# Attention and two expert layers on one core: POOL normalises with a one-input operation and rounds two weights itself

## The chip, the cores and the metric

The kernel runs on one core of a Trainium2 chip. Times are device microseconds (us) of that core. The engines are TensorE (PE in the profile; PEld is its weight load), VectorE (DVE), ScalarE (ACT), GpSimd (POOL) and SyncE (SP), which here only issues DMAs. Of the kernel before, three runs were timed; of every kernel one execution was also recorded by the hardware profiler, and that one has its own time.

## What is computed

The reference works in float32 on shapes that don't change (2 batches, 12 heads, 448 positions, 64 values a head, 896 tokens of 768):

```
scores = q @ k.T / sqrt(64), causal mask, minus the row's maximum
attn   = exp(scores);  attn = attn / (sum(attn) + 1e-9)
x      = attn @ v, heads side by side            # 896 x 768
h      = ((x @ w1) * (x @ w2)) @ w3              # 896 x 1024
x2     = h @ w_out                               # 896 x 768
h2     = x2 @ w_in;  g = h2 * clip(h2 + 3, 0, 6) / 6
out    = g @ w_out2
```

All weights arrive as 64-bit floats and are turned into 32-bit ones on the chip.

## The kernel before

[...]

**Weights.** A unit of a weight is fetched by one DMA as pairs of 32-bit words (`fetch`). `bits` makes a float32 of each pair: ACT scales the high word (line 270), DVE shifts the low word (line 277) and joins the two in two operations (lines 279 and 281). The result lies in the low word's place, so every second 32-bit word is a result. `split` then has ACT round it to `hi` (line 252) and has DVE or POOL subtract for `lo` (line 255). For the names in `POOLED`, `wr` (8 units of 128x768, the first `w_out`) and `w3` (8 units of 128x1024), the subtraction is POOL's.

**Attention.** Twelve units of two heads run first. For each, PE makes seven blocks of scores with 64 to 448 columns (line 407), DVE masks them and takes the row's extreme (line 410), ACT takes the exponential with its row sum (line 414), DVE adds 1e-9 and inverts the sums in three groups of rows (lines 425 and 426; the groups are the blocks of 448 and 384, of 320 and 256, and of 192, 128 and 64 columns), POOL multiplies each block by its inverse (line 433), PE transposes (line 455), ACT and DVE copy out of PSUM (lines 463 and 467), PE multiplies by v (line 480), and ACT and DVE split the result (lines 497 and 498). Line 433 is a `tensor_tensor` whose second operand is one value for each partition, repeated along the row.

**Beside it.** The product of `w3` and the first `w_out` (`weights_product`, called pw: 8 parts of 48 matmuls of 128x384, line 543) doesn't depend on attention. Its matmuls have a rank behind all of attention's and fill PE's gaps; what is left runs after attention. The products of x with w1 and w2 (line 686), by Strassen's scheme, come next, then lines 760, 625 and 801.

**Order.** Nothing in the program is issued as it is written. Each step is handed to `Plan` with an engine, a cost from a formula of the number of columns, what it reads and writes, and a rank. `Plan.issue` plays the engines forward by these costs and issues, on whichever engine is free, the step of lowest rank that is ready. A changed cost, or a step on another engine, therefore moves instructions on all engines. Every engine then works its queue in order, and semaphores hold it where it is early.

```
    def act(n, sb=False):
        return (0.29 if sb else 0.16) + n * 0.000833
    def dve(n):
        return 0.155 + n * 0.00104
    def pool(n):
        return 0.15 + n * 0.0023
```

Of the kernel before, what the change touches and what calls it, by code (L numbers as in the profile page):

```python
# [154 lines left out]
def attention_moe_moe2(ctx: ExitStack, tc, q, k, v, w1, w2, w3, w_out, v_in, v_out, out):  # L155
# [64 lines left out]
# [6 lines that stand above are left out]
    def pool(n):  # L226
        return 0.15 + n * 0.0023

    def fetch(plan, n, rank):
        if n >= len(units):  # L230
            return
        w, kt, m, name = units[n]
        size = kt * P
        if name == "w2":
            raw = plan.tile(lambda: later["t"].tile([P, KD * P, 2], U32, tag="raw2", name=f"{name}r{m}", bufs=2),
                            "raw2", 2, (done,))
            raw2s.append(raw)
        else:
            raw = plan.tile(lambda: ws.tile([P, KF * P, 2], U32, tag="raw", name=f"{name}r{m}", bufs=RAWS), "raw", RAWS)
        raws[n] = (raw, size)  # L240
        flat = lambda: raw[:, :size].rearrange("p f t -> p (f t)")
        if name == "wp":
            plan.op("sp", size * 0.0015, lambda: nc.sync.dma_start(flat()[:, :size], product_of[m].bitcast(U32)),
                    reads=[made], writes=[raw], rank=rank)
        else:
            plan.op("sp", size * 0.0029, lambda: nc.sync.dma_start(flat(), w[m].bitcast(U32)),
                    writes=[raw], rank=rank)

    def split(plan, hl, at_, size, x, reads, rank, eng="dve"):

        key = ("h", at_)
        plan.op("act", act(size, True), lambda: nc.scalar.copy(hl[:, HI, at_:at_ + size], x()),
                reads=reads, writes=[hl.at(("h", at_))], rank=rank)
        e = nc.gpsimd if eng == "pool" else nc.vector
        plan.op(eng, pool(size) if eng == "pool" else dve(size), lambda: e.tensor_tensor(  # L255
            hl[:, LO, at_:at_ + size], x(), f32(hl[:, HI, at_:at_ + size]), ALU.subtract),
            reads=[*reads, hl.at(("h", at_))], writes=[hl.at(("l", at_))], rank=rank)
# [1 line left out]
    def parts(name, m):  # L259
        return plan.tile(lambda: ws.tile([P, 2, KF * P], F32R, tag="hl", name=f"{name}{m}", bufs=HLS), "hl", HLS)  # L260

    def bits(plan, raw, size, rank, shifted=False):

        hi = lambda: raw[:, :size, 1]
        lo = lambda: raw[:, :size, 0]
        hb, lb = raw.at("h"), raw.at("l")

        plan.op("act", act(size, True), lambda: nc.scalar.mul(hi().bitcast(F32), hi().bitcast(F32), 2.0 ** -112),  # L270
                writes=[hb], rank=rank)
        if shifted:
            plan.op("act", act(size, True), lambda: nc.scalar.activation(
                lo(), lo(), AF.Copy, bias=THIRD[1], scale=THIRD[0]), writes=[lb], rank=rank)
        else:
            plan.op("dve", 0.16 + size * 0.00052,
                    lambda: nc.vector.tensor_single_scalar(lo(), lo(), 29, ALU.logical_shift_right),
                    writes=[lb], rank=rank)
        plan.op("dve", dve(size), lambda: nc.vector.scalar_tensor_tensor(  # L279
            lo(), hi(), 3, lo(), ALU.logical_shift_left, ALU.bitwise_or), reads=[hb], writes=[lb], rank=rank)  # L280
        plan.op("dve", dve(size), lambda: nc.vector.scalar_tensor_tensor(  # L281
            lo(), hi(), 0x80000000, lo(), ALU.bitwise_and, ALU.bitwise_or), reads=[hb], writes=[lb], rank=rank)

    def convert(plan, n, rank):
        if n >= len(units):
            return
        w, kt, m, name = units[n]
        if name == "w1":
            return
        raw, size = raws.pop(n)  # L290
        if name == "w2":
            combine(plan, m, raws.pop(n - 1)[0], raw, rank)
            return
        if name == "wr":
            hl = plan.tile(lambda: wrp.tile([P, 2, KD * P], F32R, tag="wr", name=f"wr{m}", bufs=KF), "wr", KF)
        else:
            hl = parts(name, m)
        hls[n] = hl
        if name == "wp":
            x = lambda: f32(raw[:, :].rearrange("p f t -> p (f t)")[:, :size])  # L300
            split(plan, hl, 0, size, x, [raw], rank)
            return
        bits(plan, raw, size, rank)
        split(plan, hl, 0, size, lambda: f32(raw[:, :size, 0]), [raw.at("l")], rank,
              "pool" if name in POOLED else "dve")

    def combine(plan, f, r1, r2, rank):

# [110 lines left out]
    def normalise(u, t0, t1):  # L419
# [10 lines left out]
        def scale(t):  # L430
            n = (t + 1) * T
            s = pb[:, OFF[t]:OFF[t] + n]
            nc.gpsimd.tensor_tensor(s, s, sm[:, 1, t:t + 1].to_broadcast([P, n]), ALU.mult)  # L433

        for t in reversed(range(t0, t1)):
            plan.op("pool", pool((t + 1) * T), lambda t=t: scale(t),
                    reads=[sm.at((1, t))], writes=[pb.at(t)], rank=rank)


# [431 lines left out]
```

## Time and profile before

| | |
|---|---|
| median of 3 runs | 581.37 us (580.28 to 582.85) |
| the profiled execution | 580.64 us |
| its span, first to last instruction | 578.9 us |
| PE busy | 555.5 us, 96% |
| DVE busy | 401.4 us, 69% |
| ACT busy | 294.5 us, 51% |
| POOL busy | 150.2 us, 26% |
| mean granted clock of TensorE | 0.994 |

The busy times are unions of instructions, so they can't exceed a stretch's length. They are averages over stages that are limited by different engines: POOL has work in the first half alone, and almost all of it in attention. Matmuls overlap one another, so the mean time of one is longer than the time that it adds. Where an engine's operation is held inside the hardware, not by a semaphore, the profile shows a longer operation and no wait.

### The profile page before, as it was taken

Reading aid. Unit: us, or ns where it says so; the run is one execution under the profiler, and the core shown is the slowest. Engines: PE = TensorE matmul, PEld = TensorE weight load, DVE = VectorE, ACT = ScalarE, POOL = GpSimd, SP = SyncE. Lnnn points to the kernel's source line nnn. Section 1 sums busy time; section 2 is a strip of 40 time slices with the busy share of each in tenths; the row PEclk is TensorE's granted clock in tenths of the full one; section 3 lists DMA queues with packets and bytes.
Section 4 is the critical chain, followed back from the end, with each engine's and each line's share of the span. In section 5 each row is a group of like instructions: output and inputs, shape, how many; then the busy total and the mean of one; then the engine's idle time right before and its main releaser. Section 6 shows DMA issues by size and latency. Waiting matters only on the chain.

```text
span 578.9 us, 7881 instructions
## 1 busy us (share of the span) xinstructions
PE 555.5 (96%) x2900; PEld 493.8 (85%) x2900; DVE 401.4 (69%) x675; ACT 294.5 (51%) x548; POOL 150.2 (26%) x143
## 2 busy tenths in 40 slices
PE   7697979899999999999999999999999999999997
PEld 5465656678899999889999999999999999999996
DVE  5979898897794799999736357877878855361000
ACT  5777778777673576665514335555555623130100
POOL 3968787697131243332100000000000000000000
PEclk9889999999999999999999999999999999999999
DMA  8655565543432233431413204333344442430000
GB/s 329 218 176 176 200 233 205 178 166 130 134 113 64 93 120 127 143 133 44 140 60 110 84 25 163 110 109 110 110 145 146 145 162 89 173 110 16 17 32 33
DMA packets 22855, 73.39 MB, mean 127 GB/s; under 512 B 2080, under 2 KB 11296, under 8 KB 20256
## 3 DMA queue, kind: packets, MB, share of 16 engines
q1 hardware_dynamic: 22816, 72.88, 36.6%
q8 instruction: 23, 0.38, 0.3%
q14 instruction: 16, 0.13, 0.1%
HBM read 66.98 MB, written 5.90 MB: 126 GB/s over the span
## 4 chain that ended last, share of the span: by engine, by line
PE 72%; DVE 16%; POOL 4%; issue 4%; DMA 2%; ACT 1%; SPq 0%; DVEq 0%; POOLq 0%; ACTq 0%
PE po L801 20%; PE pg L625 20%; PE px L760 10%; PE pw L543 9%; POOL prb L433 4%; PE s L407 3%; PE ptp L455 3%; PE paX L686 3%; DVE wd L255 2%; PE o L480 2%; DVE z L410 2%; DVE w1r L279 2%; PE paZ L686 1%; DMA ks<-in_k 1%; PE paY L686 1%
## 5 line engine op out<-in xcount | busy, mean ns | idle before, releaser
L801 PE MATMUL po<-g,vo 128*128 128x448 f32 x576 | 115.4, 362 | 0.0
L625 PE MATMUL pg<-x2t,vi 128*128 128x448 f32 x576 | 115.4, 362 | 0.0
L625 PEld LDWEIGHTS pg<-x2t,vi 128*128 128x128 f32 x576 | 108.0, 187 | 7.2
L801 PEld LDWEIGHTS po<-g,vo 128*128 128x128 f32 x576 | 108.0, 187 | 7.2
L433 POOL TENSOR_TENSOR prb<-prb,sums 128x448 f32<-128x448 f32 (+6 forms) x84 | 74.3, 911 | 27.5 <-DVE sums L426 25.3
L543 PE MATMUL pw<-wr,w 128*128 128x384 f32 x384 | 76.1, 347 | 0.5 <-POOL wr L255 0.5
L543 PEld LDWEIGHTS pw<-wr,w 128*128 128x128 f32 x384 | 65.9, 188 | 2.5 <-POOL wr L255 0.7
L407 PE MATMUL s<-ks,qs 128*128 128x448 f32 (+6 forms) x168 | 49.8, 405 | 10.5 <-DVE sums L410 9.8
L760 PE MATMUL px<-ab,wp 128*128 128x448 f32 x288 | 57.9, 362 | 0.0
L760 PEld LDWEIGHTS px<-ab,wp 128*128 128x128 f32 x288 | 54.0, 187 | 3.6
L414 ACT ACTIVATE prb<-z,sums 128x448 f32<-128x448 f32 (+6 forms) x84 | 42.3, 509 | 7.2 <-DVE sums L410 7.1
L407 PEld LDWEIGHTS s<-ks,qs 128*128 128x128 f32 x168 | 27.5, 192 | 19.3 <-DVE sums L410 14.2
L410 DVE CUSTOM_DVE_ANT_0 z<-s,maskb 128x448 f32<-128x448 f32 (+6 forms) x84 | 32.9, 418 | 11.5 <-PE s L407 7.3
L646 ACT ACTIVATE r<-pg,consts 128x448 f32<-128x448 f32 x32 | 20.3, 635 | 33.2 <-PE pg L625 33.2
L455 PEld LDWEIGHTS ptp<-ident,prb 128*128 128x128 f32 x192 | 23.0, 146 | 13.6 <-POOL prb L433 8.6
L455 PE MATMUL ptp<-ident,prb 128*128 128x128 f32 x192 | 27.8, 288 | 6.1 <-POOL prb L433 6.1
L270 ACT ACTIVATE vor<-vor 128x1024 f32<-128x1024 f32 x12 | 13.9, 1162 | 38.7 <-DMA vor<-in_moe_w_out 38.7
L463 ACT COPY pt<-ptp 128x512 f32<-128x512 f32 (+1 forms) x48 | 25.1, 563 | 16.0 <-PE ptp L455 15.8
L320 POOL TENSOR_TENSOR w2r<-w2r 128x384 f32<-128x384 f32 x8 | 11.4, 1431 | 77.7 <-DVE w2r L281 68.5
L648 DVE SCALAR_TENSOR_TENSOR g<-r,pg 128x448 f32<-128x448 f32 x32 | 19.8, 618 | 12.8 <-ACT r L646 12.6
L661 DVE COPY out<-po 128x448 f32<-128x448 f32 x6 | 3.8, 627 | 35.7 <-PE po L801 35.7
L659 ACT COPY out<-po 128x448 f32<-128x448 f32 x6 | 3.2, 536 | 46.1 <-PE po L801 28.3
(110 smaller groups left out, 922.6 us busy)
## 6 DMA issues: line engine op xcount, KB each, us to landing
vir<-in_moe_w_in SPq DMA_DIRECT2D x16, 768.0 KB, 4.2
vor<-in_moe_w_out SPq DMA_DIRECT2D x12, 1024.0 KB, 4.9
w3r<-in_moe_w SPq DMA_DIRECT2D x8, 1024.0 KB, 5.6
wrr<-in_moe_w_out SPq DMA_DIRECT2D x8, 768.0 KB, 4.9
w1r<-in_moe_w SPq DMA_DIRECT2D x8, 768.0 KB, 5.6
w2r<-in_moe_w SPq DMA_DIRECT2D x8, 768.0 KB, 4.3
qs<-in_q SPq DMA_DIRECT2D x12, 448.0 KB, 3.6
vr<-in_v SPq DMA_DIRECT2D x12, 256.0 KB, 2.7
```

Of the source, the lines that this page charges most:

```text
L407: plan.op("pe", pe4(n), lambda: nc.tensor.matmul(ps[:, :n], qs[u][:, t].rearrange("p h i -> p (h i)"), ks[u][:, :n], start=True, stop=True ...
L410: plan.op("dve", dve(n) + 0.09, lambda: nc.vector.tensor_tensor_reduce(out=z[:, :n], in0=ps[:, :n], in1=maskb[:, S - n:], scale=-SCALE, sc ...
L414: plan.op("act", act(n, True) + 0.2, lambda: nc.scalar.activation(pb[:, OFF[t]:OFF[t] + n], z[:, :n], AF.Exp, bias=sm[:, 0, t:t + 1], scal ...
L433: nc.gpsimd.tensor_tensor(s, s, sm[:, 1, t:t + 1].to_broadcast([P, n]), ALU.mult)
L455: nc.tensor.transpose(ps[:w, i * P:(i + 1) * P], pb[:, OFF[t] + kb * P:OFF[t] + kb * P + w], ident)
L463: plan.op("act", act(cut), lambda: nc.scalar.copy(dst()[:, :cut], ps[:, :cut]), reads=[ps], writes=[d.at((g, 0))], rank=rank)
L543: nc.tensor.matmul(ps[:, :W], weight(n, a, kk), hls[1 + kk][:, c, h * W:(h + 1) * W], start=kk == 0 and a == c, stop=kk == KF - 1 and a == LO)
L625: nc.tensor.matmul(ps[:, :S], weight(n, a, kk), x(kk, c), start=st, stop=sp)
L646: plan.op("act", act(S), lambda: nc.scalar.activation(r[:, :], ps[:, :S], AF.Relu, bias=three, scale=1.0), reads=[ps], writes=[r], rank=DE ...
L686: nc.tensor.matmul(ps[:, :S], hl[:, a, off + kk * P:off + (kk + 1) * P], t[:, c], start=first and kk == 0 and a == c, stop=kk == HK - 1 an ...
L760: nc.tensor.matmul(ps[m, b][:, :S], weight(n, a, kk), ab[kk][:, c, cols(b)], start=kk == 0 and a == c, stop=kk == KF - 1 and a == LO)
L801: nc.tensor.matmul(ps[:, :S], weight(n, a, kk), gt[k][:, c, cols(b)], start=k == 0 and a == c, stop=k == KF2 - 1 and a == LO)
```

## The change

Three things change together. The normalisation of line 433 becomes a `tensor_scalar` on POOL: one tensor, one value for each partition, a second factor of 1.0. For `w3` and `wr` POOL also makes `hi`, by a `tensor_scalar` that multiplies by 1.0 twice and writes float32r, in place of ACT's copy. And for these two weights the last operation of `bits` writes its results side by side at the start of the unit's buffer, not in every second word, so POOL reads dense rows. A cost formula `single` for both new operations enters the planner. Line numbers after line 228 shift by 3 to 14.

```diff
+    def single(n):
+        return 0.27 + n * 0.00085
+
...
     def split(plan, hl, at_, size, x, reads, rank, eng="dve"):
 
-        key = ("h", at_)
-        plan.op("act", act(size, True), lambda: nc.scalar.copy(hl[:, HI, at_:at_ + size], x()),
+        if eng == "pool":
+            plan.op("pool", single(size), lambda: nc.gpsimd.tensor_scalar(
+                hl[:, HI, at_:at_ + size], x(), 1.0, 1.0, ALU.mult, ALU.mult),
                 reads=reads, writes=[hl.at(("h", at_))], rank=rank)
+        else:
+            plan.op("act", act(size, True), lambda: nc.scalar.copy(hl[:, HI, at_:at_ + size], x()),
+                    reads=reads, writes=[hl.at(("h", at_))], rank=rank)
...
+    def flat(raw):
+        return raw[:, :].rearrange("p f t -> p (f t)")
...
+        to = (lambda: flat(raw)[:, :size]) if packed else lo
         plan.op("dve", dve(size), lambda: nc.vector.scalar_tensor_tensor(
-            lo(), hi(), 0x80000000, lo(), ALU.bitwise_and, ALU.bitwise_or), reads=[hb], writes=[lb], rank=rank)
+            to(), hi(), 0x80000000, lo(), ALU.bitwise_and, ALU.bitwise_or),
+            reads=[] if packed else [hb], writes=[lb, hb] if packed else [lb], rank=rank)
...
-        bits(plan, raw, size, rank)
-        split(plan, hl, 0, size, lambda: f32(raw[:, :size, 0]), [raw.at("l")], rank,
-              "pool" if name in POOLED else "dve")
+        pooled = name in POOLED
+        bits(plan, raw, size, rank, packed=pooled)
+        split(plan, hl, 0, size, lambda: f32(flat(raw)[:, :size] if pooled else raw[:, :size, 0]),
+              [raw.at("l")], rank, "pool" if pooled else "dve")
...
-            nc.gpsimd.tensor_tensor(s, s, sm[:, 1, t:t + 1].to_broadcast([P, n]), ALU.mult)
+            nc.gpsimd.tensor_scalar(s, s, sm[:, 1, t:t + 1], 1.0, ALU.mult, ALU.mult)
 
         for t in reversed(range(t0, t1)):
-            plan.op("pool", pool((t + 1) * T), lambda t=t: scale(t),
+            plan.op("pool", single((t + 1) * T), lambda t=t: scale(t),
                     reads=[sm.at((1, t))], writes=[pb.at(t)], rank=rank)
```

The order moves with it. On POOL, in the third unit of attention (prb is the block of exponentials that is normalised, wr the split unit of w_out, wrr its fetched words), the kernel before has

```order
L255 TENSOR_TENSOR wr_329<-wrr_173,wr_329 128x768
L433 TENSOR_TENSOR prb_87<-prb_87,sums_271 128x448
L433 TENSOR_TENSOR prb_87<-prb_87,sums_271 128x384
L433 TENSOR_TENSOR prb_87<-prb_87,sums_271 128x320
L433 TENSOR_TENSOR prb_87<-prb_87,sums_271 128x256
L255 TENSOR_TENSOR wr_397<-wrr_211,wr_397 128x768
```

and the changed kernel has

```order
L255 TENSOR_SCALAR wr_333<-wrr_173 128x768
L262 TENSOR_TENSOR wr_333<-wrr_173,wr_333 128x768
L447 TENSOR_SCALAR prb_87<-prb_87,sums_260 128x448
L447 TENSOR_SCALAR prb_87<-prb_87,sums_260 128x384
L447 TENSOR_SCALAR prb_87<-prb_87,sums_260 128x320
L447 TENSOR_SCALAR prb_87<-prb_87,sums_260 128x256
L447 TENSOR_SCALAR prb_87<-prb_87,sums_260 128x192
L447 TENSOR_SCALAR prb_87<-prb_87,sums_260 128x128
L447 TENSOR_SCALAR prb_87<-prb_87,sums_260 128x64
L255 TENSOR_SCALAR wr_444<-wrr_211 128x768
L262 TENSOR_TENSOR wr_444<-wrr_211,wr_444 128x768
```

Each split is now two POOL operations, the rounding right ahead of the subtraction, and the second split of w_out stands behind the whole unit of attention, not inside it.

On PE, at the end of attention (o is the product with v, ptp the transposes, w the split unit of w3), the kernel before has

```order
L455 MATMUL ptp_3_1603<-ident,prb_88 64x128
L480 MATMUL o_1610<-pt_1585,vr_1243 64x448 x2
L480 MATMUL o_1610<-pt_1585,vr_1243 64x320 x2
L543 MATMUL pw_1_1550<-wr_850,w_1200 128x384 x3
L480 MATMUL o_1610<-pt_1585,vr_1243 64x192 x2
L480 MATMUL o_1610<-pt_1585,vr_1243 64x64 x2
L543 MATMUL pw_1_1550<-wr_861,w_1200 128x384 x3
L543 MATMUL pw_0_1631<-wr_329,w_1309 128x384 x3
```

and the changed kernel has

```order
L557 MATMUL pw_1_1484<-wr_793,w_1134 128x384 x3
L494 MATMUL o_1542<-pt_1508,vr_1217 64x448 x2
L494 MATMUL o_1542<-pt_1508,vr_1217 64x320 x2
L494 MATMUL o_1542<-pt_1508,vr_1217 64x192 x2
L494 MATMUL o_1542<-pt_1508,vr_1217 64x64 x2
L557 MATMUL pw_1_1484<-wr_860,w_1134 128x384 x3
L557 MATMUL pw_1_1484<-wr_930,w_1134 128x384 x3
L557 MATMUL pw_0_1564<-wr_333,w_1197 128x384 x3
```

Before, the last attention matmul stands in the fourth part of pw, behind 186 of its 384 matmuls; now it stands in the third part, behind 138. ACT's queue loses 16 rows, the copies of line 252 for wr and w3.

## Rows read from the trace of the kernel before

**Rows 1.** Busy time (and instructions) of each engine by stretch.

```profile
core 0: us, PE busy (x) PEld busy (x) DVE busy (x) ACT busy (x) POOL busy (x), PEclk, DMA share, GB/s
9.60:150.30 140.70, 123.96 (x728) 89.72 (x729) 122.62 (x311) 106.59 (x265) 107.96 (x99) 0.98 0.55 186
150.30:184.30 34.00, 34.00 (x196) 33.99 (x197) 27.74 (x35) 18.42 (x32) 9.38 (x5) 1.00 0.37 117
184.30:271.20 86.90, 85.81 (x425) 79.07 (x423) 79.49 (x103) 55.40 (x90) 27.31 (x18) 1.00 0.34 113
271.20:578.90 307.70, 304.07 (x1519) 284.67 (x1519) 168.53 (x217) 110.39 (x155) 2.50 (x2) 1.00 0.28 99
```

**Rows 2.** The chain of waits in order of time: start, us, what.

```profile
150.26 34.00 PE pw L543 x195
```

**Rows 3.** The chain of waits from 9.6 to 150.3 us, shares by line.

```profile
by line: POOL prb L433 14.8%; PE pw L543 13.9%; PE s L407 12.3%; PE ptp L455 12.1%; PE o L480 8.4%; issue 8.3%; DVE z L410 7.2%; DVE sums L425 3.7%; DVE wrr L281 3.1%; DVE wrr L277 2.3%; DVE wrr L279 2.2%; DVE w3r L277 2.0%; POOL w L255 1.9
```

**Rows 4.** Waits of DVE from 9.6 to 150.3 us: us in total, times, longest.

```profile
DVE z L410 <- ACT prb L414: 4.2, 6, 1.2
DVE pt L467 <- ACT pt L463: 4.1, 5, 1.0
DVE xt L498 <- ACT xt L497: 3.5, 2, 2.6
DVE w3r L279 <- ACT w3r L270: 1.4, 3, 0.8
DVE wrr L279 <- ACT wrr L270: 1.2, 3, 0.8
```

**Rows 5.** Single undisturbed normalisations: busy us, ns of one, idle before.

```profile
L433 POOL TENSOR_TENSOR prb<-prb,sums 128x448 f32<-128x448 f32 x1 | 0.9, 934 | 0.1
...
L433 POOL TENSOR_TENSOR prb<-prb,sums 128x192 f32<-128x192 f32 x1 | 0.5, 508 | 0.6 <-DVE sums L426 0.6
L433 POOL TENSOR_TENSOR prb<-prb,sums 128x128 f32<-128x128 f32 x1 | 0.4, 401 | 0.0
L433 POOL TENSOR_TENSOR prb<-prb,sums 128x64 f32<-128x64 f32 x1 | 0.3, 295 | 0.0
```

**Rows 6.** One-input operations on POOL in the setup, groups by shape.

```profile
L388 POOL TENSOR_SCALAR_AFFINE_SELECT maskb<-maskb 64x448 f32<-64x448 f32 x2 | 1.1, 557 | 0.1
...
masks.py:199 POOL TENSOR_SCALAR_AFFINE_SELECT ident<-ident 128x128 f32<-128x128 f32 x1 | 0.3, 295 | 0.1
```

**Rows 7.** ACT's roundings of w3 and w_out, groups by shape.

```profile
L252 ACT CAST w<-w3r 128x1024 fp32r<-128x1024 f32 x8 | 9.3, 1159 | 0.4 <-DVE w3r L281 0.3
...
L252 ACT CAST wr<-wrr 128x768 fp32r<-128x768 f32 x8 | 7.4, 921 | 2.7 <-DVE wrr L281 2.7
```

**Rows 8.** A POOL split and the DVE operation that met it, in order of time.

```profile
27.01 1.84 POOL L255 TENSOR_TENSOR wr<-wrr,wr 128x768 fp32r<-128x768 f32 x1
...
27.26 2.41 DVE L281 SCALAR_TENSOR_TENSOR wrr<-wrr 128x768 uint32<-128x768 uint32 x1
```

**Rows 9.** DVE's operations on w_out (wrr), on w_in in later stages (vir), and the subtraction.

```profile
L279 DVE SCALAR_TENSOR_TENSOR vir<-vir 128x768 uint32<-128x768 uint32 x16 | 15.3, 957 | 3.9 <-ACT vir L270 3.8
L281 DVE SCALAR_TENSOR_TENSOR vir<-vir 128x768 uint32<-128x768 uint32 x16 | 15.3, 956 | 0.2
...
L281 DVE SCALAR_TENSOR_TENSOR wrr<-wrr 128x768 uint32<-128x768 uint32 x8 | 11.4, 1423 | 0.0
...
L279 DVE SCALAR_TENSOR_TENSOR wrr<-wrr 128x768 uint32<-128x768 uint32 x8 | 10.0, 1245 | 1.3 <-ACT wrr L270 1.2
...
L277 DVE TENSOR_SCALAR vir<-vir 128x768 uint32<-128x768 uint32 x16 | 9.0, 561 | 12.0 <-DMA vir<-in_moe_w_in 11.9
...
L277 DVE TENSOR_SCALAR wrr<-wrr 128x768 uint32<-128x768 uint32 x8 | 8.6, 1081 | 0.7 <-DMA wrr<-in_moe_w_out 0.7
...
L572 DVE TENSOR_TENSOR xt<-xt,bf 128x448 f32<-128x448 f32 x3 | 1.9, 619 | 0.0
```

More of the change, by code (lines that the diff above doesn't have):

```diff
@@ L260, in parts, with bits @@
         return plan.tile(lambda: ws.tile([P, 2, KF * P], F32R, tag="hl", name=f"{name}{m}", bufs=HLS), "hl", HLS)
-    def bits(plan, raw, size, rank, shifted=False):
+    def flat(raw):
+        return raw[:, :].rearrange("p f t -> p (f t)")
+    def bits(plan, raw, size, rank, shifted=False, packed=False):
         hi = lambda: raw[:, :size, 1]
@@ L299, in convert @@
         if name == "wp":
-            x = lambda: f32(raw[:, :].rearrange("p f t -> p (f t)")[:, :size])
+            x = lambda: f32(flat(raw)[:, :size])
             split(plan, hl, 0, size, x, [raw], rank)
             return
-        bits(plan, raw, size, rank)
-        split(plan, hl, 0, size, lambda: f32(raw[:, :size, 0]), [raw.at("l")], rank,
-              "pool" if name in POOLED else "dve")
+        pooled = name in POOLED
+        bits(plan, raw, size, rank, packed=pooled)
+        split(plan, hl, 0, size, lambda: f32(flat(raw)[:, :size] if pooled else raw[:, :size, 0]),
+              [raw.at("l")], rank, "pool" if pooled else "dve")
     def combine(plan, f, r1, r2, rank):
```

## The prediction

> **What bounds the kernel now.** I read the busy time by stretch first, then the chain of waits, then the waits of VectorE (DVE), last the single operations. The stretches [rows 1] show where time can be won at all. From 150.3 us on TensorE (PE) is busy without a gap: 34.00 of 34.00 us to 184.3, 85.81 of 86.90 to 271.2, and 304.07 of 307.70 to the end, and the change touches nothing there but the last w3 units. In the attention stage, 9.6 to 150.3 us, PE is busy for 123.96 of 140.70 us, so 16.7 us stand empty. DVE is busy for 122.62 (87%), POOL for 107.96 (77%), ScalarE (ACT) for 106.59 (76%). No engine is full: the stage is a pipeline of short hand-overs, and DVE and PE are nearest to their limits.
>
> The matmuls of the weights product (pw) are filler in this stage. They have the lowest rank, and what isn't done by the end of attention is done alone: 195 of the 384 in one piece of 34.00 us [rows 2], 0.174 us each. The 189 before it are 32.9 us of PE's time. **PE's total work is fixed, so the end moves only by PE's empty time in the stage.** A shorter attention with less filler in it wins nothing by itself.
>
> The chain inside the stage [rows 3] gives POOL's normalisation 14.8% of 140.7 us (20.8 us), the pw filler 13.9% (19.6 us), and the DVE lines together 20.5% (28.8 us). The listed waits of DVE on ACT in the stage make 14.4 us [rows 4].
>
> **The change part by part.** All sums are against the profiled execution, 580.64 us with a span of 578.9; it lies 0.7 us under the median of 581.37, and I carry the difference over to the median.
>
> *A, the filler.* The order of PE has 186 pw matmuls ahead of the last attention matmul before, and 138 now. The 48 at 0.174 us are 8.4 us of PE's work that moves behind attention: **+8.4**. All that follows must pay this back.
>
> *B, the filler off the chain.* Of the 32.9 us of filler, 19.6 (60%) lie on the chain, where they keep attention's own matmuls waiting in PE's queue. The same share of 8.4 us comes off attention: **-5.0**. Ends: 0, if these 48 stood in empty slots, and -8.4.
>
> *C, the normalisation.* Undisturbed, one operation takes 0.934 us at 448 elements and 0.295 at 64 [rows 5], a straight line, so the seven of a unit take 7 x (0.934 + 0.295) / 2 = 4.30 us. No row has a one-input tensor operation with a scalar on POOL. The nearest is AFFINE_SELECT, one tensor in and one out: 0.557 us at 448 and 0.295 at 128 [rows 6], hence 0.19 + 0.00082 n, and 2.80 us a unit. The dearest end is no gain, 4.30. The change's own planner assumes 0.27 + 0.00085 n, 3.41 us. Two arithmetic steps and a scalar for each partition should not be cheaper than the select, so I take 3.1, between the two. A saving of 1.2 us in 12 units is 14.4 us of POOL, but only the chain counts. The last group of a unit (192, 128 and 64) saves least: 1.20 us now, 1.0 by the same middle, 16%; all seven save 28%. About half of POOL's pieces on the chain are last groups. I take 20% of 20.8 us: **-4.2**. Ends: 0 (no gain) and -7.3 (the select's price, 35%).
>
> [...]
>
> *D, ACT without the roundings.* 8 casts at 1.159 us and 8 at 0.921 [rows 7] leave ACT, 16.7 us, of which 15.5 lie in the stage: 15% of its 106.59. They stood in ACT's queue among the exponentials and the copies out of PSUM that DVE waits for. I let the 14.4 us of waits shrink by as much: **-2.1**. Ends: 0 and -14.4.
>
> *E, rounding on POOL.* By the middle of the two prices 768 elements take 0.87 us and 1024 take 1.09, so 16 of them are 15.7 us. POOL gives up 14.4 and gets 15.7: its total stays. On the path from DVE's last bit operation to hi and lo, 0.87 replaces 0.921 and 1.09 replaces 1.159, with a hand-over between engines less: **0**. The dear end, the price of the lo subtraction beside it (1.84 us at 768 [rows 8]), would add nearly 1 us to a 768 rounding and stands in the range as rival 2. Writing side by side costs DVE nothing that a row shows; each of the 16 operations still reads two inputs.
>
> *F, DVE work that moves out.* In DVE's order two 128x768 operations of w1 (0.956 each, the same operation as the vir row in [rows 9]) and three 128x448 subtractions (0.619) leave the stage: 3.8 us. DVE is on the chain for 20.5%: **-0.8**. They land in the stretch after 150.3, where DVE has 6.3 us free [rows 1] and which grows by the moved filler.
>
> *G, DVE and POOL in each other's way.* [...] The 24 bit operations of w_out cost 0.467, 0.520 and 0.288 us more than the same operations on vir [rows 9]: 10.2 us. POOL's total stays, so I book 0; rival 2 is the other end.
>
> [...]
>
> Sum: 8.4 - 5.0 - 4.2 - 2.1 - 0.8 = **-3.7 us**, 577.7 against the median.
>
> **The rivals.** About 0.5%, 2.9 us, is what a measurement of this kernel can tell from no change.
>
> *1, DVE is the bound (slower).* For it: DVE's 87%, and nothing in the change takes work from it. Then attention shortens only by the 3.8 us that leave DVE, the moved filler is not paid back, and the end is 8.4 - 3.8 = +4.6 us, 586.0. It decides if the stage gets shorter by less than 8.4 us. Against it: 14.4 us of DVE's empty time waits for ACT, which is relieved.
>
> *2, the roundings hold DVE back (slower).* In POOL's order each rounding stands right ahead of its split. If POOL keeps DVE out through both, a hold of 1.84 us becomes 2.7, 1.5 times as long: it is met 1.5 times as often and waited for 1.5 times as long. 10.2 us would become about 22. With between half and all of the 11.5 us on the path, the sum is +2 to +8, say +5: 586.4. It decides once the extra waits pass 3.7 us. Against it: DVE gets its turn between POOL's normalisations, which also run back to back.
>
> *3, no difference.* If the select's rows flatter the price, C is 1.2 us, and if ACT was waited for only in passing, D is about 1: 8.4 - 5.0 - 1.2 - 1 - 0.8 = +0.4, 581.8.
>
> *4, more than forecast.* C at its end (7.3) and half of DVE's waits on ACT gone (7.2): 8.4 - 5.0 - 7.3 - 7.2 - 0.8 = -11.9, 569.5.
>
> **How the numbers follow.** The forecast has 0.42, of which 0.28 lies beyond -2.9 us and 0.14 within. Rival 1 has 0.15, rival 2 0.10 (0.09 slower, 0.01 within), rival 3 0.20 (0.16 within, 0.02 to each side), rival 4 0.13. Faster: 0.28 + 0.13 + 0.02 = 0.43. Same: 0.14 + 0.01 + 0.16 = 0.31. Slower: 0.15 + 0.09 + 0.02 = 0.26. The range goes from 571, which leaves out most of rival 4, to 586.5, which holds rival 1 and the middle of rival 2.
>
> **What would show it.** Right, if POOL's undisturbed one-input operation takes 0.56 to 0.65 us at 448, if the piece of pw alone at the end of attention has about 243 matmuls (42 us), and if attention ends some 12 us earlier, at about 138 us. It is rival 1 if attention ends near 146 and DVE's waits on ACT only change their names. It is rival 2 if DVE's bit operations of w_out and w3 get longer on average than [rows 9]. I am wrong altogether if time moves behind 184 us, or if the one-input operation takes over 0.934 us at 448.

## The result and the profile after

The changed kernel takes **584.33 us** (median of 11 runs, 583.12 to 585.75) against 581.18 us of the kernel before in the same job. The ratio is 1.0057, 95% interval 1.0045 to 1.0069: slower by 3.3 us. The forecast was 577.7. The profiled execution took 584.69 us with a span of 582.8, 3.9 us over the span before.

The stretches of the changed kernel, columns as in [rows 1]: attention, the pw matmuls left behind it, the two later stages.

```profile
9.60:144.80 135.20, 116.19 (x677) 80.51 (x678) 120.35 (x309) 90.45 (x246) 112.24 (x112) 0.97 0.55 188
144.80:188.10 43.30, 43.12 (x248) 42.79 (x249) 35.18 (x39) 19.73 (x35) 15.64 (x8) 1.00 0.38 119
188.10:275.00 86.90, 85.68 (x425) 79.03 (x423) 78.85 (x102) 55.16 (x90) 27.31 (x18) 1.00 0.33 113
275.00:582.80 307.80, 304.20 (x1520) 284.74 (x1519) 168.44 (x218) 110.77 (x155) 2.50 (x2) 1.00 0.29 99
```

Behind the pw piece nothing moved: 86.90 + 307.80 = 394.7 us, where it was 86.90 + 307.70 = 394.6 [rows 1]. Attention ends at 144.75 us, 5.5 us earlier than the 150.26 of [rows 2], not the 12 that I forecast, and the filler behind it takes 9.3 us longer (43.30 for 34.00). In the stage PE stands empty for 135.20 - 116.19 = 19.0 us; before it was 16.7. The filler itself went as the order said, in PE's timeline from the end of attention (start, us, engine, line, operation, tiles):

```profile
144.68 17.96 PE L557 MATMUL pw<-wr,w 128*128 128x384 f32 x102
162.82 25.23 PE L557 MATMUL pw<-wr,w 128*128 128x384 f32 x144 [0.18 <-ACT g L563]
```

These are 246 matmuls, where 195 were left before.

The new operation is as cheap as hoped. Single operations from 51.6 to 54.3 us (POOL groups by shape):

```profile
L447 POOL TENSOR_SCALAR prb<-prb,sums 128x448 f32<-128x448 f32 x1 | 0.6, 639 | 0.0
L447 POOL TENSOR_SCALAR prb<-prb,sums 128x320 f32<-128x320 f32 x1 | 0.5, 532 | 0.0
L447 POOL TENSOR_SCALAR prb<-prb,sums 128x256 f32<-128x256 f32 x1 | 0.5, 482 | 0.0
```

and from 83.5 to 88.7 us:

```profile
L255 POOL TENSOR_SCALAR w<-w3r 128x1024 fp32r<-128x1024 f32 x1 | 1.0, 1045 | 0.0
...
L447 POOL TENSOR_SCALAR prb<-prb,sums 128x64 f32<-128x64 f32 x1 | 0.3, 313 | 0.0
```

With 639 ns at 448 elements and 313 at 64 on a straight line, seven of a unit take 7 x (0.639 + 0.313) / 2 = 3.33 us, where they took 4.30 [rows 5]. Over the whole program, though, the same shapes mean this, first in the changed kernel:

```profile
L447 POOL TENSOR_SCALAR prb<-prb,sums 128x448 f32<-128x448 f32 x12 | 13.4, 1115 | 7.8 <-DVE sums L440 7.4 <-ACT prb L428 0.4
L447 POOL TENSOR_SCALAR prb<-prb,sums 128x128 f32<-128x128 f32 x12 | 11.6, 968 | 0.0
```

and then before:

```profile
L433 POOL TENSOR_TENSOR prb<-prb,sums 128x448 f32<-128x448 f32 x12 | 16.8, 1397 | 13.3 <-DVE sums L426 12.9
...
L433 POOL TENSOR_TENSOR prb<-prb,sums 128x128 f32<-128x128 f32 x12 | 9.0, 746 | 0.0
```

The 128-element operation went from 401 to about 367 ns undisturbed, and from 746 to 968 on average, of which 601 are beyond what it takes undisturbed. The sum of all 84 operations fell only from 76.6 to 70.1 us (5.84 a unit).

The waits of PE show where that hurts. In the stage (us in total, times, longest), before:

```profile
PE s L407 <- DVE sums L410: 9.8, 8, 2.2
PE ptp L455 <- POOL prb L433: 6.1, 7, 1.5
```

and after:

```profile
PE ptp L469 <- POOL prb L447: 11.8, 7, 4.2
PE s L421 <- DVE sums L424: 4.7, 5, 1.5
```

The transposes wait for POOL 5.7 us longer, although POOL's operation got shorter; the scores wait 5.1 us less for DVE. In the chain of the stage POOL's normalisation rose from 14.8% [rows 3] to:

```profile
by line: POOL prb L447 20.1%; issue 12.1%; PE s L421 11.8%; PE ptp L469 10.7%; PE o L494 10.4%; PE pw L557 7.9%; DMA wrr<-in_moe_w_out 5.9%; DVE sums L439 2.9%; DVE z L424 2.9%; POOL w L255 2.3%; DVE w3r L287 2.1%; DVE wrr L287 1.9%; DVE wr
```

20.1% of 135.2 us is 27.2 us, and pw fell from 13.9% to 7.9%: the filler left the chain as forecast, and POOL took its place.

The longest stop, 4.18 us, is in the last unit of attention. The timelines there, POOL first:

```profile
124.29 1.06 POOL L255 TENSOR_SCALAR w<-w3r 128x1024 fp32r<-128x1024 f32 x1 [1.76 <-PE pw L557]
125.44 3.24 POOL L262 TENSOR_TENSOR w<-w3r,w 128x1024 fp32r<-128x1024 f32 x1
128.65 7.84 POOL L447 TENSOR_SCALAR prb<-prb,sums 128x448 f32<-128x448 f32 x7
```

DVE beside it:

```profile
124.37 2.06 DVE L289 SCALAR_TENSOR_TENSOR w3r<-w3r 128x1024 uint32<-128x1024 uint32 x1
126.46 3.29 DVE L293 SCALAR_TENSOR_TENSOR w3r<-w3r 128x1024 uint32<-128x1024 uint32 x1
...
129.88 0.40 DVE L439 TENSOR_TENSOR sums<-sums,consts 128x3 f32<-128x3 f32 x1
...
130.40 0.98 DVE L287 TENSOR_SCALAR w3r<-w3r 128x1024 uint32<-128x1024 uint32 x1
131.48 1.36 DVE L289 SCALAR_TENSOR_TENSOR w3r<-w3r 128x1024 uint32<-128x1024 uint32 x1
```

and PE:

```profile
129.80 0.81 PE L494 MATMUL o<-pt,vr 128*64 128x192 f32 x8
130.54 1.83 PE L557 MATMUL pw<-wr,w 128*128 128x384 f32 x9
136.54 1.35 PE L469 MATMUL ptp<-ident,prb 128*128 128x128 f32 x8 [4.18 <-POOL prb L447]
137.54 2.27 PE L557 MATMUL pw<-wr,w 128*128 128x384 f32 x6
```

POOL needs 7.84 us for seven operations that take 3.33 alone. PE has work for 3.7 us of that (128.65 to 132.37). Then the transposes are next in its queue, and more than 240 filler matmuls stand behind them. At least 150 of these need nothing more from POOL: six of w3's eight units are split by 128.68 us, all of w_out's are, and the other two units of w3 belong to 96 matmuls. Right behind the stop the granted clock is 0.51 for 3.5 us (from 128 to 137.2 us it was 1.00):

```profile
137.20:140.70 3.50, 3.50 (x16) 3.40 (x14) 0.38 (x1) 1.98 (x3) 0.00 (x0) 0.51 0.00 0
```

### The profile page after: what moved, and what is told of

The parts are those of the page before. It is cut to its first block, busy times and chain, and to the rows that moved or that the text cites. A ratio compares the mean times of both kernels' runs of the same rounds, so it can differ in the third digit from the quotient of the medians.

```text
span 582.8 us, 7905 instructions
## 1 busy us (share of the span) xinstructions
PE 556.5 (95%) x2900; PEld 492.9 (85%) x2900; DVE 404.8 (69%) x675; ACT 279.3 (48%) x532; POOL 160.7 (28%) x159
## 4 chain that ended last, share of the span: by engine, by line
PE 70%; DVE 15%; POOL 6%; issue 5%; DMA 3%; ACT 1%; SPq 0%; POOLq 0%; DVEq 0%; ACTq 0%
PE po L815 20%; PE pg L639 20%; PE px L774 10%; PE pw L557 6%; POOL prb L447 5%; PE s L421 3%; PE paX L700 3%; PE ptp L469 2%; PE o L494 2%; DVE wd L262 2%; DVE w1r L289 1%; DMA wrr<-in_moe_w_out 1%; PE paZ L700 1%; DVE T L593 1%; DMA w1r<-in_moe_w 1%
## 5 line engine op out<-in xcount | busy, mean ns | idle before, releaser
L447 POOL TENSOR_SCALAR prb<-prb,sums 128x448 f32<-128x448 f32 (+6 forms) x84 | 68.8, 835 | 16.6 <-DVE sums L440 12.5
L424 DVE CUSTOM_DVE_ANT_0 z<-s,maskb 128x448 f32<-128x448 f32 (+6 forms) x84 | 33.0, 416 | 14.6 <-PE s L421 8.9
L469 PE MATMUL ptp<-ident,prb 128*128 128x128 f32 x192 | 26.8, 280 | 11.9 <-POOL prb L447 11.8
L477 ACT COPY pt<-ptp 128x512 f32<-128x512 f32 (+1 forms) x48 | 25.1, 562 | 20.8 <-PE ptp L469 20.7
L280 ACT ACTIVATE vor<-vor 128x1024 f32<-128x1024 f32 x12 | 13.9, 1160 | 36.3 <-DMA vor<-in_moe_w_out 36.3
L662 DVE SCALAR_TENSOR_TENSOR g<-r,pg 128x448 f32<-128x448 f32 x32 | 19.7, 617 | 10.5 <-ACT r L660 10.4
L494 PE MATMUL o<-pt,vr 128*64 128x448 f32 (+3 forms) x192 | 26.6, 395 | 0.0
```

The costliest lines, as they stand in the source:

```text
L424: plan.op("dve", dve(n) + 0.09, lambda: nc.vector.tensor_tensor_reduce(out=z[:, :n], in0=ps[:, :n], in1=maskb[:, S - n:], scale=-SCALE, sc ...
L447: nc.gpsimd.tensor_scalar(s, s, sm[:, 1, t:t + 1], 1.0, ALU.mult, ALU.mult)
L469: nc.tensor.transpose(ps[:w, i * P:(i + 1) * P], pb[:, OFF[t] + kb * P:OFF[t] + kb * P + w], ident)
L477: plan.op("act", act(cut), lambda: nc.scalar.copy(dst()[:, :cut], ps[:, :cut]), reads=[ps], writes=[d.at((g, 0))], rank=rank)
L494: nc.tensor.matmul(ps[T * j:T * j + T, kb * P:S], vr[u][:w, kb, j, :], d[:w, base[kb]:base[kb] + TQ - 2 * kb, j, :], start=kb == 0, stop=k ...
```

## The experiments

All edits are against the changed kernel unless the text says otherwise. The kernel before had medians of 581.0 to 581.8 us in these jobs; ratios are to the kernel before in the same job, and 0.1% is 0.58 us.

### The parts one at a time

**n_same.** The kernel before with one edit, the one-input normalisation. It is planned at the old price, so every engine's order is that of before.

```diff
-            nc.gpsimd.tensor_tensor(s, s, sm[:, 1, t:t + 1].to_broadcast([P, n]), ALU.mult)
+            nc.gpsimd.tensor_scalar(s, s, sm[:, 1, t:t + 1], 1.0, ALU.mult, ALU.mult)
```

> The kernel before with the one-input normalisation alone, planned at the old price, so that every engine's order is that of the kernel before and only the 84 POOL operations differ. Theory O (the order: the rounding on POOL makes the plan take 51 filler matmuls out of attention, which the real stage does not pay back; the normalisation itself is a gain): 1 to 3 us faster than before, POOL's undisturbed operation 0.64 us at 448. Theory L (the lock between DVE and POOL: shorter POOL operations are only blocked more often, so nothing is won): within 1 us of before, POOL's 84 operations busy about 74 us as before.

575.49 us, ratio 0.9894 (0.9870 to 0.9917). The operation alone, with nothing else moved, wins 6.2 us, twice what theory O allowed; theory L (within 1 us, the 84 operations at about 74 us) is out, they took 65.9. Its stretch of attention, columns as in [rows 1]:

```profile
9.60:145.70 136.10, 124.78 (x728) 89.42 (x728) 112.88 (x314) 106.87 (x265) 99.22 (x99) 0.97 0.57 196
```

PE stands empty for 11.3 us (16.7 before). DVE's busy time fell from 122.62 [rows 1] to 112.88 us, though DVE does the same work in the same order; what differs is POOL's 84 operations, 65.9 us where they took 76.6. DVE's operation of L281 on w_out took 988 ns on average, where [rows 9] have 1423 and the one in [rows 8], which met a split of POOL, took 2410.

**n_new.** As n_same, but with the new price for the normalisation; the rounding stays on ACT.

```diff
...
-            plan.op("pool", pool((t + 1) * T), lambda t=t: scale(t),
+            plan.op("pool", single((t + 1) * T), lambda t=t: scale(t),
```

> The kernel before with the one-input normalisation, planned at its new price, rounding still on ACT. The order has 189 filler matmuls ahead of the last attention matmul, as before. Theory O: 1 to 4 us faster than before. Theory L: within 1 us of before.

576.0 us, ratio 0.9911 (0.9885 to 0.9937), no different from n_same by its interval and 1 us better than theory O's bound. The new price is harmless where ACT rounds, although PE waits longer for POOL than in n_same (4.5 us):

```profile
PE ptp L458 <- POOL prb L436: 8.1, 9, 2.2
```

No stop there is longer than 2.2 us.

**r_only.** Rounding on POOL and results side by side, as in the change, but the two-input normalisation at its old price.

```diff
-            nc.gpsimd.tensor_scalar(s, s, sm[:, 1, t:t + 1], 1.0, ALU.mult, ALU.mult)
+            nc.gpsimd.tensor_tensor(s, s, sm[:, 1, t:t + 1].to_broadcast([P, n]), ALU.mult)
...
-            plan.op("pool", single((t + 1) * T), lambda t=t: scale(t),
+            plan.op("pool", pool((t + 1) * T), lambda t=t: scale(t),
```

> Rounding on POOL from results side by side alone; the normalisation stays the two-input operation at its old price. The order has 144 filler matmuls ahead of the last attention matmul (189 before). Theory O: the whole loss and more, 4 to 7 us slower than before, attention's end at most 5 us earlier. Theory L: 3 to 5 us slower, with DVE's three bit operations on w3 and w_out longer on average than in the kernel before.

582.89 us, ratio 1.0025 (1.0010 to 1.0040): the rounding, with the order that it draws, costs 1.5 us, less than either theory said. In attention DVE is busy for 128.74 us, 6.1 more than before:

```profile
9.60:145.10 135.50, 118.09 (x683) 83.07 (x683) 128.74 (x311) 92.40 (x247) 123.89 (x114) 0.96 0.56 189
```

**a_oldcost.** Every operation of the change; only the planned price of the normalisation is the old one.

```diff
-            plan.op("pool", single((t + 1) * T), lambda t=t: scale(t),
+            plan.op("pool", pool((t + 1) * T), lambda t=t: scale(t),
```

> The changed kernel with the normalisation planned at the old price: the same order on every engine as the kernel with rounding alone, and only the 84 POOL operations are one-input. Theory O: 1 to 3 us faster than that kernel, 1 to 4 us slower than before. Theory L: within 1 us of that kernel.

**574.96 us, ratio 0.9890 (0.9868 to 0.9911)**, faster than both kernels: 9.7 us faster than the changed kernel with the same operations. Neither theory had this: O said 1 to 4 us slower than before, L within 1 us of r_only, and it is 7.8 us faster than r_only. Its order is that of r_only, so 45 of the 51 filler matmuls are moved here too (240 are left). Attention ends at 135.67 us, 14.6 earlier than before. Its stage, and PE's two longest waits in it:

```profile
9.60:135.70 126.10, 115.47 (x685) 81.06 (x684) 118.32 (x311) 92.19 (x249) 116.75 (x114) 0.99 0.60 202
```

```profile
PE s L421 <- DVE sums L424: 4.1, 7, 1.5
PE ptp L469 <- POOL prb L447: 3.2, 3, 1.8
```

PE stands empty for 10.6 us, 8.4 less than in the changed kernel; the waits for POOL's normalisation alone are 8.6 us less. POOL isn't less busy for it: the 84 operations take 74.3 us here and 70.1 in the changed kernel. (2.7 us of the changed kernel's empty time are a wait for the first DMA of k that a_oldcost's profile lacks. Before and n_same, which have one order, have 0.6 and 2.7 us there, so that part goes with the execution, not with the order.) The last unit goes like this on POOL and then on PE:

```profile
121.24 8.29 POOL L447 TENSOR_SCALAR prb<-prb,sums 128x448 f32<-128x448 f32 x7
```

```profile
124.65 0.33 PE L494 MATMUL o<-pt,vr 64*64 64x64 f32 x4 [0.77 <-DVE pt L481]
124.91 2.87 PE L557 MATMUL pw<-wr,w 128*128 128x384 f32 x15
129.58 1.09 PE L469 MATMUL ptp<-ident,prb 128*128 128x128 f32 x8 [1.80 <-POOL prb L447]
```

POOL's seven take as long as in the changed kernel (8.29 us for 7.84). The difference is what PE has in its queue ahead of the transposes: but for one wait of 0.77 us it has work until 127.78, 6.5 us from POOL's start, where it had 3.7.

**a_tt.** The changed kernel's exact order, with the two-input normalisation (the first line of r_only's edit, alone).

> The changed kernel with its exact order, but the normalisation is the two-input operation again: 0.96 us more for a unit undisturbed, 11.5 us in all. If POOL's normalisation is what this order waits for (theory A), at least half of it shows: 590 to 596 us, PE's waits for POOL 16 us or more. If PE stands for other reasons and POOL only happens to be named (rival B), 584 to 587 us.

591.59 us, ratio 1.0178 (1.0156 to 1.0201), in the time that theory A forecast. The wait was a little under its 16 us:

```profile
PE ptp L469 <- POOL prb L447: 14.5, 8, 4.8
```

Four kernels now make a square, in ratios to the kernel before; all four round on POOL:

| | two-input normalisation | one-input | the operation |
|---|---|---|---|
| order of the old price | r_only 1.0025 | a_oldcost 0.9890 | -1.35%, 7.8 us |
| order of the new price | a_tt 1.0178 | the change 1.0057 | -1.21%, 7.0 us |
| **the order** | +1.53%, 8.9 us | +1.67%, 9.7 us | |

The operation wins 7 to 8 us in either order, and the order that the new price draws costs 9 to 10 us with either operation. The two add up.

### What in the new price's order costs so much

**p_eps, p_mid, p_flat.** The changed kernel with 0.02, 0.12 and 0.25 us added to the planned price of each normalisation. The last gives a unit 5.16 us, the old price's sum, but flat over the shapes.

```diff
-            plan.op("pool", single((t + 1) * T), lambda t=t: scale(t),
+            plan.op("pool", single((t + 1) * T) + 0.02, lambda t=t: scale(t),
```

> The changed kernel with the normalisation planned 0.02 us dearer an operation; instructions are the same, the order differs in some places (132 filler matmuls ahead of the last attention matmul, 138 in the changed kernel). Theory P (a cheap planned price, far below the 0.84 us that an operation takes on average between DVE's holds, makes the plan systematically bad): 582 to 586 us, as the changed kernel. Theory F (the changed kernel's order is one unlucky draw, and orders scatter by several us whatever the price): anywhere from 574 to 586, most likely under 581.

> As above with 0.12 us more an operation, half of the way to the old price (135 filler matmuls). Theory P: between, 578 to 581 us. Theory F: no trend, 574 to 584.

> As above with 0.25 us more an operation, so that a unit's seven cost 5.16 us in the plan, the sum of the old price (144 filler matmuls). Theory P: 574 to 577 us, as the changed kernel with the old price. Theory F: no trend, 574 to 584.

p_eps: 584.19 us, ratio 1.0060 (1.0040 to 1.0080). p_mid: 579.45, 0.9972 (0.9944 to 1.0000). p_flat: 580.32, 1.0004 (0.9969 to 1.0038). A hair on the price changes the order but not the time, so the changed kernel's order is no single accident. PE's waits for POOL's normalisation fall with the price, from 11.8 us over 9.6 and 7.9 to 3.5. The time falls too, but not in step: p_mid's runs go from 576.3 to 582.5 us and p_flat's from 577.5 to 585.5, so the order of these two is not settled. Their scatter goes with the granted clock: p_mid's fastest run had a mean clock of 0.997 and its slowest 0.988, p_flat's 0.994 and 0.981. p_eps and p_mid lie where theory P put them; p_flat does not (574 to 577 us), though its prices add up to the old ones. Its 3.5 us are one stop, in the last unit again, and the eight transposes behind it took 1.97 us, as they do in p_tail (below), where the granted clock was 0.51 in that stretch; in a_oldcost, at 1.00, they took 1.09:

```profile
132.86 1.97 PE L469 MATMUL ptp<-ident,prb 128*128 128x128 f32 x8 [3.51 <-POOL prb L447]
```

From POOL's start on that unit PE had 5.0 us of work (3.7 in the changed kernel, 6.5 in a_oldcost).

**p_real.** The same, planned at 1.13 times the old formula: 5.85 us a unit, what POOL really took in the changed kernel, holds included.

```diff
-            plan.op("pool", single((t + 1) * T), lambda t=t: scale(t),
+            plan.op("pool", 1.13 * pool((t + 1) * T), lambda t=t: scale(t),
```

> The changed kernel with the normalisation planned at 1.13 times the old formula, 5.85 us for a unit of seven, which is what POOL really took on average in the changed kernel, holds included. Theory A: as good as the old price, 573 to 579 us, PE's waits for POOL at most 4.5 us. Rival B (the old price happens to draw a good order, and another price draws any other): 578 to 585 us.

585.06 us, ratio 1.0052 (1.0032 to 1.0071). Theory A is wrong here on the time: the price that matches the real mean is as slow as the price that is far too low. It was right on the wait for POOL, of which nothing is left among PE's waits in the stage. Another took its place:

```profile
PE s L421 <- DVE sums L424: 17.5, 11, 3.2
PE s L421 <- DMA ks<-in_k: 1.9, 1, 1.9
PE ptp L469 <- ACT pt L477: 0.3, 1, 0.3
```

Now the scores wait for DVE, which has to read the earlier ones out of PSUM. So the price is not a thing to set to the truth: it moves the wait between POOL and DVE. Why DVE is late in this order I did not follow up.

**lat.** All prices as in the change, but the plan believes that POOL's results reach the other engines 0.6 us after the operation, not 0.12.

```diff
-    LATENCY = {"pe": 0.2, "sp": 2.2}
+    LATENCY = {"pe": 0.2, "sp": 2.2, "pool": 0.6}
```

> The changed kernel with its prices, but the plan believes that a result of POOL reaches other engines 0.6 us later (0.12 before). Theory A (the new price lets the plan put PE's transposes into PE's queue before POOL delivers, and filler stands behind them): PE's waits for POOL's normalisation in the stage fall from 11.8 us to under 6, PE stands empty in the stage for 11 to 15 us in place of 19.0, and the time is 574 to 580 us. Rival B (the order is slow by chance, or POOL paces the stage whatever stands in PE's queue): waits stay at 8 us or more and the time at 582 to 586.

577.22 us, ratio 0.9933 (0.9908 to 0.9958), 7.2 us better than the change, with PE empty for 13.4 us in the stage and this wait:

```profile
PE ptp L469 <- POOL prb L447: 5.4, 6, 1.8
```

Time, wait and empty time are all in theory A's bounds. No work and no price was touched; only when the plan lets other engines follow POOL, PE's transposes above all, but also the filler that reads POOL's splits.

**p_ends and p_tail.** The new price for the first nine units and the old for the last three, and the other way round.

```diff
-            plan.op("pool", single((t + 1) * T), lambda t=t: scale(t),
+            plan.op("pool", (single if u < 9 else pool)((t + 1) * T), lambda t=t: scale(t),
```

> The new price for the first nine units of attention, the old one for the last three. Theory E (most of the loss is the stop of PE in the last unit and the half clock behind it): no stop over 2 us and no fall of the granted clock after 115 us, PE empty in the stage for 13 to 15.5 us, time 577 to 580.5 us. Rival S (the loss is spread evenly over the twelve units, 0.7 us each): three of twelve units are mended, 581 to 583 us.

> The old price for the first nine units of attention, the new one for the last three, the complement of the run before it. Theory E (the loss sits where the last units meet the w3 splits): a stop of PE at the transposes of over 2 us after 115 us, PE empty in the stage for 14 us or more, 579 to 584 us. Rival S (the loss is spread over the units): nine of twelve units are mended, 576 to 578.5 us, and no stop over 2 us.

p_ends: 577.83 us, ratio 0.9939 (0.9921 to 0.9956), no stop over 1.9 us, the granted clock at 1.00 from 110 to 150 us, PE empty for 12.5 us, a little less than theory E asked. p_tail: 581.93 us, ratio 0.9993 (0.9972 to 1.0015), with the stop back in the last unit, and a granted clock of 0.51 for 6.9 us from the middle of the stop on (its empty time, 13.6 us, is just under E's 14):

```profile
131.07 1.97 PE L469 MATMUL ptp<-ident,prb 128*128 128x128 f32 x8 [3.12 <-POOL prb L447]
```

```profile
129.90:136.80 6.90, 5.73 (x24) 5.60 (x25) 2.18 (x4) 2.68 (x5) 1.12 (x1) 0.51 0.00 0
```

Taking the new price from the last three units wins 1.18% (6.9 us) on the change; giving it to them alone costs 1.03% (6.0 us) on a_oldcost. So about two thirds of the 9.7 us are lost there, and theory S, with three twelfths, falls. Half of it may be the clock: by an estimate, 6.9 us at 0.51 lose 3.4 us, and PE's empty time in p_tail is 3.0 us over a_oldcost's. p_tail's two runs with a mean clock of 0.997 or more took 577.9 and 578.4 us, its seven at 0.991 or less 580.6 to 582.7. One thing in p_tail speaks against the queue alone as the cause of the stop: PE had 7.1 us of work from POOL's start on the last unit (120.82 to 127.95), more than in a_oldcost, but POOL took 10.2 us for the seven operations.

**w3_act.** New price, w_out rounded on POOL, w3's rounding back on ACT.

```diff
-    def split(plan, hl, at_, size, x, reads, rank, eng="dve"):
+    def split(plan, hl, at_, size, x, reads, rank, eng="dve", by="act"):
...
-        if eng == "pool":
+        if by == "pool":
...
-              [raw.at("l")], rank, "pool" if pooled else "dve")
+              [raw.at("l")], rank, "pool" if pooled else "dve", "pool" if name == "wr" else "act")
```

> The changed kernel with its new price, but w3's rounding back on ACT; w_out's stays on POOL. Theory W (the new price hurts only together with roundings of w3 on POOL, which stand ahead of the last units' normalisations): 574 to 579 us, no stop over 2 us after 115 us. Rival P (the new price alone draws the poor order): 581 to 586 us, with PE's waits for POOL at 9 us or more.

578.62 us, ratio 0.9946 (0.9923 to 0.9970): theory W. PE's waits for POOL are 6.7 us, the longest 1.2. POOL itself now pauses before each group of the last unit, so its results aren't what is late:

```profile
126.93 2.04 POOL L447 TENSOR_SCALAR prb<-prb,sums 128x192 f32<-128x192 f32 x3 [2.37 <-DVE sums L440]
129.52 2.46 POOL L447 TENSOR_SCALAR prb<-prb,sums 128x448 f32<-128x448 f32 x2 [0.55 <-DVE sums L440]
133.51 2.08 POOL L447 TENSOR_SCALAR prb<-prb,sums 128x320 f32<-128x320 f32 x5 [1.53 <-DVE sums L440]
```

With n_new this says that most of the new price's cost needs w3's rounding on POOL: w3_act is 6.5 us faster than the changed kernel, though still 3.3 us behind a_oldcost. The order of w3_act differs in much else (159 filler matmuls ahead of attention's end for 138), so the rounding itself, 1.05 us, and the order that comes with it are not told apart.

**ao_unp.** a_oldcost with DVE's results in every second word again, in the same order.

```diff
-        bits(plan, raw, size, rank, packed=pooled)
-        split(plan, hl, 0, size, lambda: f32(flat(raw)[:, :size] if pooled else raw[:, :size, 0]),
+        bits(plan, raw, size, rank)
+        split(plan, hl, 0, size, lambda: f32(raw[:, :size, 0]),
```

> The changed kernel with the old price of the normalisation, and DVE's last bit operation writing every second word as before, so that POOL rounds and subtracts from a strided row. Order the same as with dense rows. If dense rows are needed, POOL's rounding of 768 takes over 1 us (0.83 dense) and the kernel is 1 us or more slower than the 575.0 of that order; if the spacing costs nothing, within 1 us of it.

578.16 us, ratio 0.9933 (0.9905 to 0.9961), against a_oldcost's 0.9890: 2.5 us, and the two intervals overlap a little. Not all of it is the spacing. Three of its five runs had a mean granted clock of 0.993 or 0.994 (578.2 to 578.3 us), two had 0.997 (576.3 and 576.4), where all of a_oldcost's had 0.997 or more (574.2 to 576.7). At like clock side by side is worth 1 to 2 us, hardly more than the noise. Undisturbed, POOL's rounding of 1024 elements took 1.12 to 1.16 us from strided rows and 1.045 from dense ones; that of 768 took 0.88 to 0.92 for 0.83, dearer, but not the "over 1 us" that was expected.

## Why the prediction was wrong

**What failed** is the sum's reading of the order. I let the new order enter by one count, the moved filler (A and B), and took C to F from before's trace as if they held in any order. For all of the order I had booked 8.4 - 5.0 = 3.4 us. The runs take the change apart otherwise: the operation alone wins 6.2 us (n_same), the rounding with 45 of the moved filler matmuls adds nothing that can be told (a_oldcost is 0.2 us faster than n_same), and the order of the new price, which moves only 6 more, costs 9.7 us. By the sum's own count these 6 are worth 6 x 0.174 x 0.4 = 0.4 us. So the sum counted filler, and the loss is not in the filler. What I did not ask is what the new price lets the plan put *ahead* of the filler on PE: transposes whose input POOL delivers later than the plan believes, in the last unit 7.84 us for seven operations planned at 3.41.

- **A** was right as a count: 246 left for "about 243". The text counted 186 filler matmuls ahead of attention's last matmul; that was ahead of the last product's first one. Ahead of its last it was 189, so 51 moved, 8.9 us and not 8.4. Nor is A a loss by itself: a_oldcost moves 45 and wins.
- **B** was right in kind (pw's share of the chain fell from 19.6 us to 10.7) and empty in effect: the chain went to POOL instead, 27.2 us for 20.8.
- **C and G.** The price was 3.33 us a unit, where I took 3.1 and the planner 3.41. The gain was undersized all the same: 6.2 us in before's order (7.0 and 7.8 in the two others) for 4.2 and 0. What is missing may be G: with POOL's shorter operations DVE was busy for 9.7 us less in n_same than before, and for 10.4 less in a_oldcost than in r_only. No run separates that from a C that was sized too small.
- **D, E.** The rounding on POOL cost 1.5 us (r_only) or nothing that can be told (a_oldcost against n_same, 0.2 us better), for a forecast of -2.1. DVE's busy time rose by 6.1 and 5.4 us in the same two pairs. So the relief of ACT's queue that D booked was probably used up by that rise, a milder form of rival 2; the order differs in both pairs, so this is not shown by itself. And E's clause that writing side by side changes nothing missed 1 to 2.5 us.
- **Rival 1** gave 586.0 and "attention ends near 146", both close, but by luck: the mechanism is another. DVE is not the bound: with the same operations a_oldcost ends attention at 135.67.
- **Rival 2** went half its way. In the last unit of the changed kernel DVE got in between rounding and subtraction: its L289 ended at 126.43 us, 1.08 us behind the rounding, while the subtraction went on until 128.68 (more in the last section). So there it wasn't kept out through both. Its sign, the bit operations getting longer on average, came out mixed. For w3 before:

```profile
L281 DVE SCALAR_TENSOR_TENSOR w3r<-w3r 128x1024 uint32<-128x1024 uint32 x8 | 10.8, 1356 | 0.0
```

and in the changed kernel:

```profile
L293 DVE SCALAR_TENSOR_TENSOR w3r<-w3r 128x1024 uint32<-128x1024 uint32 x8 | 14.3, 1790 | 0.1
...
L289 DVE SCALAR_TENSOR_TENSOR wrr<-wrr 128x768 uint32<-128x768 uint32 x8 | 10.2, 1276 | 0.1
...
L293 DVE SCALAR_TENSOR_TENSOR wrr<-wrr 128x768 uint32<-128x768 uint32 x8 | 8.1, 1009 | 0.1
```

The w_out operations took 1245 and 1423 ns before [rows 9]; one stayed, one got shorter. w3's got longer, and w3 is what meets the last units. The mixture comes from the cheaper normalisation. With the same normalisation the sign is there: the three operations of a w3 unit took 3.94 us before and 4.64 in r_only, those of a w_out unit 3.75 and 3.93 (sums of the means).

So far as it is shown: the order that the new price draws costs 9.7 us, and two thirds of that sit in the last three units, where w3's splits, DVE's w3 operations and the normalisations meet. PE runs into transposes that aren't ready, with filler behind them, and a clock of 0.51 comes with it (for 3.5 us in the change, for 6.9 in p_tail). Telling the plan that POOL is late wins 7.2 of the 9.7 us back. The lower clock alone is not the cause: the changed kernel's run with a mean clock of 0.996 took 583.1 us, and a_oldcost's five at 0.997 took 574.7 to 576.7. Of the rest, some 3 us in the first nine units, p_ends shows only that PE's transposes still wait there for POOL, 5.2 us in five stops (all before 89 us). What stays open is why POOL's seven operations take 7.8 to 10.2 us in the last unit of these orders, and why DVE is late in p_real.

## What to carry to other kernels

Where a planner's costs draw the order, a cheaper operation is two changes, and each can be had without the other: run the new operation in the old order first, then let the price move. A planned price that is right for an undisturbed operation can be far from what the engine takes among its neighbours (0.64 us alone and 1.12 on average for the new operation at 448 elements), and setting it to the real mean is no cure either (p_real); two sets of prices with the same sum gave 575 and 580 us (a_oldcost, p_flat). So read which engine's waits the new order lengthens. On an engine that works its queue in order, look at what independent work stands *behind* an instruction that may wait (here more than 240 matmuls behind a wait of 4.18 us).

## What the runs showed of the hardware

- **POOL's one-input rounding and a two-input DVE operation took turns in the one stretch that was read for it**, in the changed kernel's last unit. POOL's rounding ends at 125.35 us (124.29 + 1.06). DVE's L289, begun at 124.37, ends at 126.43, 1.08 us after it; it took 2.06 us, and the fastest of its kind 1.20. POOL's subtraction, begun at 125.44, ends at 128.68, 2.25 us after that; it took 3.24, the fastest 2.36. DVE's L293, begun at 126.46, ends at 129.75, 1.07 us after that; it took 3.29, the fastest 1.19. The 1.08, 2.25 and 1.07 us behind the other's end are close to the fastest times.
- **What POOL's one-input `tensor_scalar` took in the changed kernel, undisturbed**: with one value for each partition 0.313 us at 64 elements and 0.639 at 448; the straight line through the two is 0.26 us and 0.00085 us an element. The rounding, with two constants and dense rows, took 0.83 at 768 and 1.045 at 1024, some 0.08 us under that line.
- **The granted clock was 0.51 in or right behind the stop of PE in the last unit**, in the change (a stop of 4.18 us, then 3.5 us at 0.51) and in p_tail (3.12 us, with 6.9 at 0.51). In a_oldcost, whose stop there is 1.80 us, it stayed at 1.00 from 21 to 570 us. The length of a stop doesn't settle it: p_ends had no stop over 1.8 us for POOL either, and its clock was 0.92 on average from 50 to 70 us; n_new had one of 2.2 us, and its clock was 0.94 from 9.6 to 40 us, as a_oldcost's was, and 1.00 from 40 us on.
